# Three output stores placed behind two crossbar turns, and one tile turned one output piece sooner

## The chip, the core and the metric

The kernel runs on one core of a Trainium2 chip. The metric is the device time of one execution in microseconds; lower is better. Inside the core, TensorE (PE in the profile; its weight loads are listed as PEld), VectorE (DVE), ScalarE (ACT), GpSimd (POOL) and SyncE (SP) each run their own list of instructions in order and wait for each other through semaphores. Transfers are issued by SP and POOL and carried out by 16 DMA engines.

## The reference

Causal linear attention with a decay for each head, followed by a feed-forward layer with a snake activation:

```python
gamma = 1.0 - 2.0 ** (-5.0 - np.arange(H))                 # q, k, v: (4, 8, 768, 64)
for t in range(S):
    state = gamma[None, :, None, None] * state + np.einsum('bhd,bhe->bhde', k[:, :, t], v[:, :, t])
    y[:, :, t] = (1.0 / np.sqrt(D)) * np.einsum('bhd,bhde->bhe', q[:, :, t], state)
x = y.transpose(0, 2, 1, 3).reshape(B * S, H * D)          # 3072 x 512
h = x @ w_in                                               # 512 x 2048
s = np.sin(alpha * h)
out = (h + s * s / (alpha + 1e-09)) @ w_out                # 2048 x 512
```

## The kernel before

The 3072 tokens are cut into 24 tiles of 128 tokens. `P` (the list `order`) gives their order in time: P[0] to P[3] are the first tiles of the four batches, then come the other tiles of the batches. The tiles are grouped for the feed-forward layer: group 0 is P[0] to P[3], groups 1 to 8 have two tiles each (group 1 is P[4] and P[5], group 2 is P[6] and P[7], and so on), and the last group has four.

A tile passes these steps. Its q and k rows are loaded into `qkr` and v into `vr`, by transfers that POOL issues (`load_chunk`, profile lines L101 and L103). Then q and k are turned, so that the head dimension lies on the partitions; the result is the tile `qkT`. There are two ways to turn. For P[4] to P[7], `stage_T` does it on TensorE with 16 transposes (L281) and a copy of the result out of PSUM by ACT (L283) or DVE (L285). From P[8] on, `turn` does it through the crossbar of the DMA engines (`dma_start_transpose`, issued by SP, L290). After that `burst(old, new)` works on two neighbouring tiles at once on TensorE: for the tile `old` the products with the carried state (L365), the products with the scores (L438) and the sums for the state (L445); for the tile `new` its scores (L380), which read the `qkT` of `new`. The output of `burst` goes to `xT` by DVE (L487, "exit"), and the state goes to `s_f` and `s_q`.

The feed-forward layer of a group takes `xT` as input. `Slot` multiplies a column block of `w_in` with `xT` (L603), ACT takes the sine (L606) and the square (L611), and DVE adds the two parts into `gT` (L618). `ff_out` multiplies one of the 16 slices of `gT` with `w_out` for one tile (L628); one such matmul is called an output piece below. After the sixteenth piece `take` copies the tile's output from PSUM to a buffer `o_sb` (ACT L642 or DVE L640, five buffers) and issues its store on SP (L643).

The order on every engine is written out by hand (`tc.manual_schedule`). For group 0 and the passage to group 1 it is a long list of calls: the pieces of tiles P[2] and P[3] are laid one by one (`fill(n)` puts the next n of them) between the turns and bursts of P[4], P[5] and P[6]. The lines of this place:

```python
    run(fresh, "keep", "hand", "mask")
    fill(2)
    F((0, 1), (14,))
    F((0, 1), (15,))
    run(fresh, "exit")
    ...
    fill(1)
    stage_T(P[6], nc.scalar, "mm")
    fill(3)
    run(burst(P[5], P[6]), "exit", "keep", "hand", "mask")
    fill(4)
```

Group 1 then runs in `phase(1, ...)`, where `stage_T(P[7])` stands after the first slot, the crossbar turns of P[8], P[9] and P[10] after the second, third and sixth, and the bursts P[6]/P[7] and P[7]/P[8] in the third and sixth slot. The bursts P[8]/P[9] and P[9]/P[10] stand in `phase(2, ...)`.

On SP there is one list for stores and crossbar turns. The stores of the first three tiles of group 0 that are finished (P[2], P[0], P[1]) are issued as soon as `take` is called, ahead of the turns of P[8], P[9] and P[10].

Of the kernel before, what the change touches and what calls it, by code (L numbers as in the profile page):

```python
# [12 lines left out]
AFTER = mybir.DependencyInfo(mybir.DependencyClass.Sync, mybir.DependencyReason.DATA)  # L13


@with_exitstack
def kernel(
# [116 lines left out]
    def load_w_in(i, h=None):  # L134
        c = slice(i * fw, (i + 1) * fw) if h is None else slice(i * fw + h * fw // 2, i * fw + (h + 1) * fw // 2)
        nc.gpsimd.dma_start(out=w_in[:, :, c], in_=w_in_v[:, :, c])  # L136
# [28 lines left out]
    load_chunk(0, "v")  # L165
    load_chunk(order[1])
    load_chunk(order[2])
    for h in range(2):
        load_w_in(0, h)
    tok = consts.tile([128, NCH, 2], F32, name="tok")  # L170
    for b in range(2):
        nc.gpsimd.iota(tok[64 * b:64 * b + 64], pattern=[[C, NCH], [64, 2]], channel_multiplier=1, base=0,
                       allow_small_or_imprecise_dtypes=True)
    load_chunk(order[3], "qk")
    load_w_out(0, 0)
    load_chunk(order[3], "v")
    load_w_out(0, 1)
    for h in range(2):
        load_w_in(1, h)
    for h in range(2):  # L180
        load_w_out(1, h)
        load_w_in(2, h)


# [76 lines left out]
    def half_T(j, i, eng, bank=None):  # L261
# [7 lines left out]
        if eng is nc.scalar:  # L269
            nc.scalar.copy(o, pt)  # L270
        else:
            nc.vector.tensor_copy(o, pt)

    def stage_T(j, eng=None, tag="two"):
        pt = psum.tile([128, 2 * NP, 128], BF16, name="pt", tag=tag, bufs=4 if tag == "mm" else 1)
        st["qkT", j] = work.tile([128, 2 * NP, 128], BF16, name="qkT", tag="qkT", bufs=6)
# [5 lines left out]
        if eng is nc.scalar:  # L282
            nc.scalar.copy(st["qkT", j], pt)  # L283
        else:
            nc.vector.tensor_copy(st["qkT", j], pt)  # L285
# [7 lines left out]
    def stage_A(j, parts=1):  # L293
# [7 lines left out]
        aT = st["aT", j] = work.tile([128, 2, NP, 128], BF16, name="aT", tag="aT", bufs=3)  # L301
        if parts == 1:
            nc.vector.tensor_mul(aT.rearrange("p e n t -> p (e n) t"), pa.rearrange("p e n t -> p (e n) t"),  # L303
                                 dec.rearrange("p e n t -> p (e n) t"))
            return
        for h in range(2):
            c = slice(2 * h, 2 * h + 2)
# [22 lines left out]
    def stage_M(j, bank, parts=1):  # L330

        aT, vs = st["aT", j], raw["v", j]
        py = bank.rearrange("i (p t) -> i p t", p=NP)
        for h in range(parts):
            ps = range(NP * h // parts, NP * (h + 1) // parts)
            if h:
                py = psum.tile([128, NP, 128], F32, name="pyh", tag="mm", bufs=4)
            for p in ps:
                for e in range(2):
                    nc.tensor.matmul(py[half(e), p, :], vs[:, 2 * p + e, :], aT[:, e, p, :],  # L340
                                     start=(p == ps[0]), stop=True, skip_group_check=True)
            c = slice(ps[0], ps[-1] + 1)
            (nc.scalar.copy if parts == 1 else nc.vector.tensor_copy)(x_of(j)[:, c], py[:, c])


# [243 lines left out]
    class Slot:  # L589
# [19 lines left out]
        def sq(self, eng):  # L609
            if eng == "A":  # L610
                nc.scalar.activation(out=self.s, in_=self.s, func=ACTF.Square)  # L611
            else:
                nc.vector.tensor_mul(self.s, self.s, self.s)
# [11 lines left out]
    def ff_out(g, ts, f):  # L625
# [4 lines left out]
        if f == FF - 1 and (g, ts) not in ((0, 0), (0, 1)):  # L630
            take(g, ts)

    def take(g, ts):
# [5 lines left out]
        elif g > 0 or ts == 1:  # L639
            nc.vector.tensor_copy(o_sb, po[g, ts])  # L640
        else:
            nc.scalar.copy(o_sb, po[g, ts])  # L642
# [28 lines left out]
    def idle_work(n):  # L671
        for _ in range(n):
            nc.tensor.matmul(spare["ps"], warm[:, :128], warm, start=True, stop=True)  # L673
# [6 lines left out]
    idle_work(9)  # L680
    nc.vector.tensor_copy(raw["q", 0], near["q"])
    half_T(e0, 0, nc.vector)
    nc.scalar.copy(raw["k", 0], near["k"])
    idle_work(2)
    nc.vector.tensor_mul(dec.rearrange("p e n t -> p (e n) t"), dec.rearrange("p e n t -> p (e n) t"), mask_bc)
    half_T(e0, 1, nc.scalar)
    nc.scalar.activation(out=kg, in_=expo, func=ACTF.Exp, scale=-1.0)
    for c in range(1, NCH):
        nc.scalar.activation(out=step[:, c, :], in_=lgp, func=ACTF.Exp, scale=float(C * c))
    idle_work(2)  # L690
    stage_A(e0)
    half_T(e1, 0, nc.scalar)
    grow(0)
    idle_work(1)
    half_T(e1, 1, nc.vector)
    nc.tensor.transpose(pal, alpha_row, ident_f)
    stage_M(e0, front[:, 0])
    later_tables()
    nc.scalar.copy(alpha_sb, pal)
    grow(1)  # L700
    stage_A(e1)
    nc.scalar.activation(out=kgq, in_=expoq, func=ACTF.Exp, scale=-1.0)
    idle_work(1)
    half_T(e2, 0, nc.scalar)
    grow(2)
    idle_work(2)
    half_T(e2, 1, nc.vector)
    grow(3)
    stage_M(e1, front[:, 0])
    nc.scalar.activation(out=tiny, in_=warm[:, 0:1], func=ACTF.Sin)  # L710
    stage_A(e2, 2)
    idle_work(3)
    stage_M(e2, front[:, 0], 2)
    nc.vector.tensor_scalar_add(rec_alpha, pal, 1e-9)
    nc.vector.reciprocal(rec_alpha, rec_alpha)
    idle_work(2)
    scale_v(e0, nc.vector)
    for h in range(2):
        decay_table(2 * h + 1)
        decay_table(2 * h + 2)  # L720
        load_w_out(2, h)
        load_w_in(3, h)
    load_w_out(3, 0)
    load_chunk(order[4])
    load_chunk(order[5], "qk")
    load_w_out(3, 1)
    load_chunk(order[5], "v")
    decay_table(5)
    load_chunk(order[6])


    rest = [{}]

    def phase(g, outs, att, nf=1, on_vector=(), tags={}, early=()):
# [3 lines left out]
        for n in range(FF // nf):  # L738
# [13 lines left out]
            run(fresh, *(("keep", "hand", "exit") if g == 1 else ("mask", "keep0")))  # L752
            if fresh:
                rest[0] = fresh
            while done < min(no, no * (n + 1) * nf // (FF - 2 * (g == 1))):
# [7 lines left out]
            if g == 1:  # L763
                run(fresh, "mask")
# [11 lines left out]
    def F(ts, fs):  # L776
        for f in fs:
            for t in ts:
                ff_out(0, t, f)
        if FF - 1 in fs:  # L780
            for t in ts:
                take(0, t)

    def early(f, tag="mm"):
        return Slot(0, f, (0, n3), tag=tag)

    outs = out_pieces(0, (2, 3))[6:]

    def fill(n):
        for _ in range(n):  # L790
            outs.pop(0)()

    fourth = psum.tile([128, 2, 512], BF16, name="fourth", tag="two", padded_shape=[128, 2, 1024])
    a = early(0).sq("A")
    b = early(1).sq("A")
    half_T(e3, 0, nc.vector, fourth[:, 0])
    c = early(2).sq("A")
    a.add()
    half_T(e3, 1, nc.vector, fourth[:, 1])
    d = early(3).sq("A")  # L800
    b.add()
    stage_A(e3)
    both = psum.tile([128, 2, d_model], F32, name="po", tag="two")
    po[0, 0], po[0, 1] = both[:, 0], both[:, 1]
    F((0, 1, 2), (0, 1))
    c.add()
    stage_M(e3, psum.tile([128, 2, 512], F32, name="pye", tag="pa")[:, 0])
    copies = first_state(e0)
    d.add()
    copies()  # L810
    F((0, 1, 2), (2,))
    a = Slot(0, 0, (n3, n4), 4, "pa")
    F((0, 1, 2), (3,))
    a.sq("A").add()
    a = Slot(0, 4).sq("A")
    for f in range(5, FF):
        b = Slot(0, f, tag="pa" if f in (7, 10) else "mm")
        if f % 2 == 0 or f in (7, 11, 15):
            b.sq("A")
        if f % 2 == 0 and f - 1 not in (7, 11, 15):  # L820
            a.sq("D")
        a.add()
        a = b
        if f > 6:
            F((0, 1, 2) if f < 9 else (0, 1), (f - 3,))
        if f in (7, 9, 11):
            scale_v({7: e1, 9: e3, 11: e2}[f], nc.vector)
    scale_v(P[4], nc.gpsimd)
    stage_T(P[4], nc.vector, "pa")
    F((0, 1), (13,))  # L830
    fill(3)
    a.add()
    fill(1)
    m4 = scores(P[4])["mask"]
    stage_T(P[5], nc.scalar, "mm")
    m4()
    fill(6)
    scale_v(P[5], nc.vector)
    fresh = burst(P[4], P[5], apart=True)
    run(fresh, "keep", "hand", "mask")  # L840
    fill(2)
    F((0, 1), (14,))
    F((0, 1), (15,))
    run(fresh, "exit")


    load_chunk(P[7], "qk")
    load_chunk(P[8], "qk")
    scale_v(P[6], nc.gpsimd)
    load_chunk(P[7], "v")  # L850
    load_chunk(P[9], "qk")
# [103 lines left out]
```

## Time and profile before

| | |
|---|---|
| median of 3 runs | 208.54 us (208.07 to 210.15) |
| the profiled execution: time, and span from first to last instruction | 208.83 us, 206.8 us |
| TensorE busy | 200.2 us, 97% of the span |
| DVE, ACT, POOL busy | 153.0, 152.1, 124.1 us |
| granted TensorE clock | 1.00 |
| DMA moved | 24.79 MB, mean 120 GB/s |

The profile was taken in an execution of 208.83 us, 2.03 us more than its span of 206.8 us; this rest lies outside the first and last instruction. Busy time adds up what an engine spent in instructions. A matmul's row gives its start, and the start of the next row says how long TensorE stayed with it, because matmuls overlap: the durations of matmuls are longer than the distance between their starts. The chain that ended last tells which engine's work followed which up to the end.

### The profile page before, as it was taken

Reading aid. Unit: us, or ns where it says so; the run is one execution under the profiler, and the core shown is the slowest. Engines: PE = TensorE matmul, PEld = TensorE weight load, DVE = VectorE, ACT = ScalarE, POOL = GpSimd, SP = SyncE. Lnnn points to the kernel's source line nnn. Section 1 sums busy time; section 2 is a strip of 40 time slices with the busy share of each in tenths; the row PEclk is TensorE's granted clock in tenths of the full one; section 3 lists DMA queues with packets and bytes.
Section 4 is the critical chain, followed back from the end, with each engine's and each line's share of the span. In section 5 each row is a group of like instructions: output and inputs, shape, how many; then the busy total and the mean of one; then the engine's idle time right before and its main releaser. Section 6 shows DMA issues by size and latency. Waiting matters only on the chain.

```text
span 206.8 us, 5804 instructions
## 1 busy us (share of the span) xinstructions
PE 200.2 (97%) x2367; PEld 123.7 (60%) x2367; DVE 153.0 (74%) x323; ACT 152.1 (74%) x311; POOL 124.1 (60%) x172
## 2 busy tenths in 40 slices
PE   7699999999999999999999999999999999999994
PEld 2345544557766666766766676766766654444453
DVE  5688499767999988878879695975978975656220
ACT  7588888656997787787787778688686779999001
POOL 8998987999799996899486909990220000000000
PEclk9999999999999999999999999999999999999999
DMA  8999999999999999999995999992412101010212
GB/s 128 153 182 192 201 200 173 167 199 181 122 167 120 101 175 178 172 135 156 170 143 60 122 110 139 123 144 59 105 52 53 55 0 52 0 51 3 101 51 101
DMA packets 102906, 24.79 MB, mean 120 GB/s; under 512 B 93360, under 2 KB 99936, under 8 KB 102880
## 3 DMA queue, kind: packets, MB, share of 16 engines
q0 software_dynamic: 80080, 13.38, 89.8%
q1 hardware_dynamic: 22656, 10.99, 25.4%
q8 instruction: 18, 0.29, 0.6%
q10 hardware_dynamic: 144, 0.07, 0.1%
q14 instruction: 8, 0.07, 0.1%
HBM read 27.30 MB, written 6.29 MB: 162 GB/s over the span
## 4 chain that ended last, share of the span: by engine, by line
PE 88%; ACT 4%; DMA 3%; DVE 2%; issue 1%; SPq 0%
PE po L628 39%; PE ph L603 38%; DMA o_sb<-in_k_dram 3%; PE poh L653 2%; ACT s L606 2%; PE py L365 1%; ACT s L611 1%; PE pt L281 1%; PE py L429 1%; PE pa L380 1%; DVE gT L618 1%; DVE aT L308 1%; DVE aT L303 1%; PE pa L387 1%; PE pa L299 1%; PE py L438 1%
## 5 line engine op out<-in xcount | busy, mean ns | idle before, releaser
L618 DVE SCALAR_TENSOR_TENSOR gT<-s,rec_alpha,ph 128x256 bf16<-128x256 f32 (+3 forms) x164 | 79.8, 522 | 29.2 <-ACT s L611 28.8
L603 PE MATMUL ph<-xT,w_in 128*128 128x256 bf16 (+3 forms) x656 | 98.6, 291 | 0.3 <-DVE gT L618 0.3
L606 ACT ACTIVATE s<-ph,alpha_sb 128x256 f32<-128x256 f32 (+3 forms) x164 | 75.9, 505 | 26.4 <-PE ph L603 23.0
L628 PE MATMUL po<-w_out,gT 128*128 128x512 bf16 x368 | 95.2, 380 | 0.0
L603 PEld LDWEIGHTS <-w_in 128*128 128x128 bf16 x656 | 63.3, 98 | 33.3 <-issue 0.9
L611 ACT ACTIVATE s<-s 128x512 f32<-128x512 f32 (+1 forms) x94 | 58.8, 625 | 3.0
L628 PEld LDWEIGHTS <-gT 128*128 128x128 bf16 x368 | 34.2, 98 | 30.2 <-DVE gT L618 0.5
L125 POOL DMA_DIRECT2D qk_seq<-in_q_dram x32 | 21.6, 760 | 3.4 <-DMA v_seq<-in_v_dram 3.4
L125 POOL DMA_DIRECT2D qk_seq<-in_k_dram x32 | 21.3, 728 | 3.7 <-DMA qk_seq<-in_q_dram 3.5
L640 DVE COPY o_sb<-po 128x512 f32<-128x512 f32 x20 | 13.8, 688 | 9.4 <-PE po L628 9.0
L125 POOL DMA_DIRECT2D v_seq<-in_v_dram x24 | 16.9, 792 | 0.2
L163 POOL TENSOR_TENSOR v_seq<-v_seq,kgq 128x512 bf16<-128x512 bf16 x10 | 10.2, 1044 | 5.0 <-DMA v_seq<-in_v_dram 5.0
L103 POOL DMA_DIRECT2D vr<-in_v_dram x11 | 10.5, 951 | 0.8 <-DMA w_in<-in_moe_w_in_dram 0.6
L399 DVE TENSOR_TENSOR aTw<-pa,maskq 128x768 bf16<-128x768 f32 x10 | 9.5, 954 | 0.0
L487 DVE TENSOR_TENSOR xT<-py,qg 128x512 bf16<-128x512 f32 x13 | 8.9, 683 | 0.6 <-PE py L445 0.6
L657 ACT COPY o_sb<-poh 128x256 f32<-128x256 f32 (+1 forms) x2 | 0.6, 318 | 11.7 <-PE poh L653 11.7
L673 PE MATMUL spare<-warm 128*128 128x512 bf16 x22 | 8.0, 485 | 1.2 <-DVE warm L186 1.2
L513 POOL CAST s_q<-s_f 128x256 bf16<-128x256 f32 x1 | 0.4, 396 | 14.2 <-DVE s_f L507 14.2
L383 DVE TENSOR_TENSOR aT<-pa,mask 128x1024 bf16<-128x1024 f32 x7 | 8.5, 1219 | 0.4 <-PE pa L380 0.4
L513 ACT CAST s_q<-s_f 128x256 bf16<-128x256 f32 x12 | 4.7, 392 | 3.1 <-DVE s_f L507 2.6
L136 POOL DMA_DIRECT2D w_in<-in_moe_w_in_dram x8 | 6.3, 800 | 0.5 <-DMA w_out<-in_moe_w_out_dram 0.5
L103 POOL DMA_DIRECT2D qkr<-in_k_dram x7 | 6.3, 896 | 0.4 <-DMA w_in<-in_moe_w_in_dram 0.4
(123 smaller groups left out, 173.0 us busy)
## 6 DMA issues: line engine op xcount, KB each, us to landing
out_dram<-o_sb SPq DMA_DIRECT2D x23, 256.0 KB, 2.5
w_in<-in_moe_w_in_dram POOLq DMA_DIRECT2D x8, 256.0 KB, 7.9
w_out<-in_moe_w_out_dram POOLq DMA_DIRECT2D x8, 256.0 KB, 7.9
vr<-in_v_dram POOLq DMA_DIRECT2D x11, 128.0 KB, 5.6
v_seq<-in_v_dram POOLq DMA_DIRECT2D x16, 80.0 KB, 4.4
qkr<-in_q_dram POOLq DMA_DIRECT2D x7, 128.0 KB, 5.9
qkr<-in_k_dram POOLq DMA_DIRECT2D x7, 128.0 KB, 6.1
qk_seq<-in_q_dram POOLq DMA_DIRECT2D x16, 48.0 KB, 3.4
```

The source lines that it names most:

```text
L103: nc.gpsimd.dma_start(out=t, in_=chunk_of(src, j))
L125: nc.gpsimd.dma_start(out=o, in_=src[bt, head(b, m, e), now[0] * C:(now[-1] + 1) * C, :].rearrange("(f i) d -> i f d", i=64))
L163: eng.tensor_mul(t, t, by[:, j % NCH, :, None].to_broadcast([128, H, D]))
L383: return {"mask": lambda: nc.vector.tensor_mul(aT.rearrange("p e n t -> p (e n) t"), pa.rearrange("p e (n t) -> p (e n) t", n=NP), mask_bc)}
L399: return {"mask": lambda: nc.vector.tensor_mul(aT, pa[:, :, 0:384].rearrange("p e (m t) -> p e m t", m=2), maskq[:, None, None, :].to_broa ...
L487: nc.vector.tensor_mul(o, st["pyw", old][:, :, 0:256].rearrange("p b (m t) -> p b m t", m=2), by)
L603: nc.tensor.matmul(self.ph[:, m, :], w_in[:, i, f * 128:(f + 1) * 128], xT[g][:, i, self.lo:self.hi], start=(m == 0 and i == 0), stop=(i = ...
L606: nc.scalar.activation(out=self.s[:, m, :], in_=self.ph[:, m, :], func=ACTF.Sin, scale=alpha_sb[:, f:f + 1])
L611: nc.scalar.activation(out=self.s, in_=self.s, func=ACTF.Square)
L618: nc.vector.scalar_tensor_tensor(gT[self.g][:, f, self.lo:self.hi], self.s[:, m, :], rec_alpha[:, f:f + 1], self.ph[:, m, :], op0=ALU.mult ...
L628: nc.tensor.matmul(po[g, ts], gT[g][:, f, ts * C:(ts + 1) * C], w_out[:, f, :], start=(f == 0), stop=(f == FF - 1))
L640: nc.vector.tensor_copy(o_sb, po[g, ts])
```

## The change

Two things move. First, the list of calls for group 0, for the passage to group 1 and for group 1 itself is replaced by a table of words, `PLAN`, which `act` carries out one by one; nearly every word stands where its call stood. `stage_T`, `half_T`, `stage_A` and `stage_M` are split so that the PSUM copy is a word of its own, and `take` no longer issues the store when it is told which engine copies; the store is the word `G`. Second, two of the words stand elsewhere: the word that turns P[6] on TensorE (`T.6.mm`) stands ahead of the piece `F.3.2`, and the stores `G.2 G.0 G.1` stand behind the crossbar turns `X.8` and `X.9`.

```diff
+PLAN = """
...
+keep.4 hand.4 mask.4 F.3.0 F.3.1 F.01.14 F.01.15 O.0.A O.1.D exit.4 L.7.q L.7.k L.8.q L.8.k V.6.P L.7.v L.9.q
+L.9.k L.8.v V.7.P L.10.q L.10.k L.9.v V.8.P T.6.mm C.6.A F.3.2 F.3.3 F.3.4 F.3.5 U.5 exit.5 keep.5 hand.5 mask.5
+F.3.6 F.3.7 F.3.8 F.3.9 S.1:0.mm Q.1:0.A T.7.two C.7.D A.1:0 S.1:1.mm Q.1:1.A X.8 F.3.10 A.1:1 S.1:2.mm Q.1:2.A
+X.9 G.2 G.0 G.1 U.6 keep.6 hand.6 exit.6 F.3.11 A.1:2 mask.6 S.1:3.mm Q.1:3.A F.3.12 A.1:3 S.1:4.mm Q.1:4.A
+F.3.13 A.1:4 S.1:5.mm Q.1:5.A U.7 X.10 keep.7 hand.7 exit.7 F.3.14 A.1:5 mask.7 S.1:6.mm Q.1:6.A F.3.15 O.3.A
+G.3 A.1:6 S.1:7.mm Q.1:7.A A.1:7
+"""
...
-    def take(g, ts):
+    def take(g, ts, by=None):
...
+        if by is not None:
+            return o_sb
         nc.sync.dma_start(out=out_view[:, groups[g][ts], :], in_=o_sb)
...
+        elif op == "F":
+            for t in a[0]:
+                ff_out(0, int(t), int(a[1]))
+        elif op == "O":
+            aside["O" + a[0]] = take(0, int(a[0]), eng(a[1]))
+        elif op == "G":
+            nc.sync.dma_start(out=out_view[:, groups[0][int(a[0])], :], in_=aside.pop("O" + a[0]))
...
+        elif op == "T":
+            aside[a[0]] = stage_T(P[int(a[0])], a[1])
+        elif op == "C":
+            aside.pop(a[0])(eng(a[1]))
+        elif op == "X":
+            turn(P[int(a[0])])
...
-    fill(1)
-    stage_T(P[6], nc.scalar, "mm")
-    fill(3)
-    run(burst(P[5], P[6]), "exit", "keep", "hand", "mask")
-    fill(4)
```

The first place is on TensorE, at the turn of P[6]. `po_412` is the output of P[1], `po_747` (now `po_746`) that of P[3], `pt` the PSUM tile of the turn, and `py` the output of the burst P[5]/P[6]. Before, the turn's 16 pairs of weight load and transpose (one pair is shown) stand behind the third piece of P[3], and three more pieces of P[3] come between it and the burst:

```order
L628 MATMUL po_412<-w_out_70,gT_355 128x512
L628 LDWEIGHTS gT_355
L628 MATMUL po_747<-w_out_70,gT_355 128x512
L281 LDWEIGHTS qkr_349
L281 MATMUL pt_866<-ident_120,qkr_349 64x128
...
L365 LDWEIGHTS s_q0_170
L365 MATMUL py_888<-qkT_652,s_q0_170 64x128
```

With the change the turn follows the last piece of P[1] directly, and four pieces of P[3] come between it and the burst:

```order
L632 MATMUL po_412<-w_out_70,gT_355 128x512
L287 LDWEIGHTS qkr_350
L287 MATMUL pt_786<-ident_91,qkr_350 64x128
...
L632 MATMUL po_746<-w_out_70,gT_355 128x512
L369 LDWEIGHTS s_q0_141
L369 MATMUL py_809<-qkT_652,s_q0_141 64x128
```

One weight load and one matmul moved from ahead of the turn to behind it; nothing else on TensorE stands elsewhere.

The second place is SP's list. `qkr_765`, `qkr_773` and `qkr_781` are the loaded q and k of P[8], P[9] and P[10] (now `qkr_762`, `qkr_770` and `qkr_778`). Before, the three stores stand ahead of all turns:

```order
L151 DMA alpha_row_79<-in_moe_alpha_dram 16x128
L643 DMA out_0_dram<-o_sb_677 128x512
L643 DMA out_0_dram<-o_sb_754 128x512
L643 DMA out_0_dram<-o_sb_757 128x512
L290 DMA_TRANSPOSE qkT_1004<-qkr_765 128x8x128
L290 DMA_TRANSPOSE qkT_1022<-qkr_773 128x8x128
L290 DMA_TRANSPOSE qkT_1197<-qkr_781 128x8x128
L643 DMA out_0_dram<-o_sb_1220 128x512
```

With the change they stand between the second and the third turn:

```order
L173 DMA alpha_row_79<-in_moe_alpha_dram 16x128
L293 DMA_TRANSPOSE qkT_925<-qkr_762 128x8x128
L293 DMA_TRANSPOSE qkT_943<-qkr_770 128x8x128
L763 DMA out_0_dram<-o_sb_677 128x512
L763 DMA out_0_dram<-o_sb_753 128x512
L763 DMA out_0_dram<-o_sb_755 128x512
L293 DMA_TRANSPOSE qkT_1121<-qkr_778 128x8x128
L763 DMA out_0_dram<-o_sb_1144 128x512
```

Two turns moved past three stores. DVE, ACT and POOL carry out the same instructions in the same order as before.

More of the change, by code (lines that the diff above doesn't have):

```diff
@@ L163, in scale_v, with number_tokens @@
         eng.tensor_mul(t, t, by[:, j % NCH, :, None].to_broadcast([128, H, D]))
[L165 to L169, printed above, removed]
-    tok = consts.tile([128, NCH, 2], F32, name="tok")
[L171 to L182, printed above, removed]
+    tok = consts.tile([128, NCH, 2], F32, name="tok")
+    def number_tokens():
+        for b in range(2):
+            nc.gpsimd.iota(tok[64 * b:64 * b + 64], pattern=[[C, NCH], [64, 2]], channel_multiplier=1, base=0,
+                           allow_small_or_imprecise_dtypes=True)
     warm = consts.tile([128, 512], BF16, name="warm")
@@ L268, in half_T, with stage_T @@
         o = st["qkT", j][:, i * NP:(i + 1) * NP, :]
[L269 to L274, printed above, removed]
+        return lambda by: by.copy(o, pt) if by is nc.scalar else by.tensor_copy(o, pt)
+    def stage_T(j, tag):
         pt = psum.tile([128, 2 * NP, 128], BF16, name="pt", tag=tag, bufs=4 if tag == "mm" else 1)
-        st["qkT", j] = work.tile([128, 2 * NP, 128], BF16, name="qkT", tag="qkT", bufs=6)
+        qkT = st["qkT", j] = work.tile([128, 2 * NP, 128], BF16, name="qkT", tag="qkT", bufs=6)
         for i in range(2):
@@ L281, in stage_T @@
                     nc.tensor.transpose(pt[half(e), i * NP + p, :], raw["qk"[i], j][:, h, :], ident)
[L282 to L285, printed above, removed]
+        return lambda by: by.copy(qkT, pt) if by is nc.scalar else by.tensor_copy(qkT, pt)
     def turn(j):
@@ L300, in stage_A, with decayed @@
                                  start=(p == 0), stop=True, skip_group_check=True)
-        aT = st["aT", j] = work.tile([128, 2, NP, 128], BF16, name="aT", tag="aT", bufs=3)
-        if parts == 1:
+        return pa
+    def decayed(j, pa, c):
+        if ("aT", j) not in st:
+            st["aT", j] = work.tile([128, 2, NP, 128], BF16, name="aT", tag="aT", bufs=3)
+        aT = st["aT", j]
+        if c.stop - c.start == NP:
             nc.vector.tensor_mul(aT.rearrange("p e n t -> p (e n) t"), pa.rearrange("p e n t -> p (e n) t"),
                                  dec.rearrange("p e n t -> p (e n) t"))
-            return
-        for h in range(2):
-            c = slice(2 * h, 2 * h + 2)
+        else:
             nc.vector.tensor_mul(aT[:, :, c], pa[:, :, c], dec[:, :, c])
@@ L328, in x_of, with mixed @@
         return xT[g][:, :, i * C:(i + 1) * C]
-    def stage_M(j, bank, parts=1):
+    def mixed(j, part, bank=None):
         aT, vs = st["aT", j], raw["v", j]
+        if bank is None:
+            bank = front[:, 0] if part != "1" else psum.tile([128, 512], F32, name="pyh", tag="mm", bufs=4)
         py = bank.rearrange("i (p t) -> i p t", p=NP)
[L334 to L343, printed above, removed]
+        ps = {"-": range(NP), "0": range(2), "1": range(2, NP)}[part]
+        for p in ps:
+            for e in range(2):
+                nc.tensor.matmul(py[half(e), p, :], vs[:, 2 * p + e, :], aT[:, e, p, :],
+                                 start=(p == ps[0]), stop=True, skip_group_check=True)
+        c = slice(ps[0], ps[-1] + 1)
+        o = x_of(j)[:, c]
+        return lambda by: by.copy(o, py[:, c]) if by is nc.scalar else by.tensor_copy(o, py[:, c])
     tiles4 = [(b, e) for b in range(2) for e in range(2)]
@@ L629, in ff_out @@
                          start=(f == 0), stop=(f == FF - 1))
-        if f == FF - 1 and (g, ts) not in ((0, 0), (0, 1)):
+        if f == FF - 1 and g > 0:
             take(g, ts)
-    def take(g, ts):
+    def take(g, ts, by=None):
         o_sb = work.tile([128, d_model], F32, name="o_sb", tag="o_sb", bufs=5)
@@ L638, in take @@
             nc.scalar.copy(o_sb[:, h:], po[g, ts][:, h:])
-        elif g > 0 or ts == 1:
+        elif by is nc.scalar:
+            nc.scalar.copy(o_sb, po[g, ts])
+        else:
             nc.vector.tensor_copy(o_sb, po[g, ts])
-        else:
-            nc.scalar.copy(o_sb, po[g, ts])
+        if by is not None:
+            return o_sb
         nc.sync.dma_start(out=out_view[:, groups[g][ts], :], in_=o_sb)
@@ L669, with idle_work @@
     spare = {"ps": psum.tile([128, 512], F32, name="spare", tag="mm", bufs=4)}
-    def idle_work(n):
+    def idle_work(n, cols=512):
         for _ in range(n):
-            nc.tensor.matmul(spare["ps"], warm[:, :128], warm, start=True, stop=True)
+            nc.tensor.matmul(spare["ps"][:, :cols], warm[:, :128], warm[:, :cols], start=True, stop=True)
     def grow(p):
@@ L679 @@
     e0, e1, e2, e3 = order[:B]
[L680 to L729, printed above, removed]
     rest = [{}]
@@ L751, in phase @@
                 now.add()
-            run(fresh, *(("keep", "hand", "exit") if g == 1 else ("mask", "keep0")))
+            run(fresh, "mask", "keep0")
             if fresh:
                 rest[0] = fresh
-            while done < min(no, no * (n + 1) * nf // (FF - 2 * (g == 1))):
+            while done < min(no, no * (n + 1) * nf // FF):
                 outs[done]()
@@ L775 @@
     n3, n4 = 3 * C, 4 * C
[L776 to L794, printed above, removed]
@@ L812 @@
[L812 to L827, printed above, removed]
@@ L828 @@
-    scale_v(P[4], nc.gpsimd)
-    stage_T(P[4], nc.vector, "pa")
-    F((0, 1), (13,))
-    fill(3)
-    a.add()
-    fill(1)
[L834 to L850, printed above, removed]
@@ L857 @@
+    for word in PLAN.split():
+        act(word)
     load_seq(1, "q")
@@ L867 @@
         scale_v(j, nc.gpsimd)
-    fill(1)
-    stage_T(P[6], nc.scalar, "mm")
-    fill(3)
-    run(burst(P[5], P[6]), "exit", "keep", "hand", "mask")
-    fill(4)
-    where = {7: (1, 2), 8: (1, 5)}
+    where = {}
     for g in range(2, 6):
@@ L888, in B @@
         return lambda: burst(old, new, first, beside=beside, second=second)
-    at((1, 0), lambda: stage_T(P[7]))
-    for n in (8, 9):
-        at((1, n - 7), X(P[n]))
-    for n in range(7, 17):
+    for n in range(9, 17):
         new = P[n]
```

149 lines of the change are left out of this document (116 added, 33 removed).

## Prediction

> **What bounds the kernel now.** I read the page first: busy times, the slices, the chain that ended last. Then the waits of TensorE from 14 us on, to see how much of its time can be won at all.
>
> ```profile
> span 206.8 us, 5804 instructions
> PE 200.2 (97%) x2367; PEld 123.7 (60%) x2367; DVE 153.0 (74%) x323; ACT 152.1 (74%) x311; POOL 124.1 (60%) x172
> PE   7699999999999999999999999999999999999994
> PE 88%; ACT 4%; DMA 3%; DVE 2%; issue 1%; SPq 0%
> ```
>
> ```profile
> PE ph L603 <- DVE gT L618: 0.3, 1, 0.3
> PE pyh L340 <- DVE aT L308: 0.2, 1, 0.2
> ```
>
> TensorE sets the time: 97% of the span, 88% of the chain, and the only slices under nine tenths are the first two and the last. The second fence is all that the view of TensorE's waits has between 14 and 205 us: 0.5 us. Nothing that the change touches lies ahead of 43 us or behind the first store after the third turn, so a gain of over 1% (2.1 us) has no idle time from which it could come. A loss needs a new wait of TensorE.
>
> **The turn of P[6].** TensorE's rows around it, then two plain pieces and two plain bursts for comparison (start, duration):
>
> ```profile
> 44.19 0.64 PE L281 MATMUL pt<-ident,qkr 128*64 128x128 bf16 x16
> 44.76 0.82 PE L628 MATMUL po<-w_out,gT 128*128 128x512 bf16 x3
> 45.51 0.31 PE L365 MATMUL py<-qkT,s_q 64*64 64x128 bf16 x8
> ...
> 46.45 1.04 PE L628 MATMUL po<-w_out,gT 128*128 128x512 bf16 x4
> 47.39 1.03 PE L603 MATMUL ph<-xT,w_in 128*128 128x256 bf16 x8
> ...
> 50.99 0.31 PE L365 MATMUL py<-qkT,s_q 64*64 64x128 bf16 x8
> ...
> 51.85 0.39 PE L628 MATMUL po<-w_out,gT 128*128 128x512 bf16 x1
> 52.07 1.04 PE L603 MATMUL ph<-xT,w_in 128*128 128x256 bf16 x8
> ...
> 58.71 1.03 PE L603 MATMUL ph<-xT,w_in 128*128 128x256 bf16 x8 [0.28 <-DVE gT L618]
> ```
>
> A burst takes from its first L365 to the piece behind it. The burst P[6]/P[7] takes 51.85 - 50.99 = 0.86 us, the burst P[5]/P[6] takes 46.45 - 45.51 = 0.94 us with the same instructions. So 0.08 us are lost inside the second, too short to be listed as a wait. The weight loads and ACT's rows say where:
>
> ```profile
> 45.50 0.14 PEld L365 LDWEIGHTS <-s_q 64*64 64x64 bf16 x8 [0.42 <-issue]
> ...
> 45.93 0.26 PEld L380 LDWEIGHTS <-qkT 64*64 64x64 bf16 x16
> ...
> 50.99 0.15 PEld L365 LDWEIGHTS <-s_q 64*64 64x64 bf16 x8 [0.21 <-ACT s L606]
> ...
> 51.22 0.12 PEld L380 LDWEIGHTS <-qkT 64*64 64x64 bf16 x2
> ```
>
> ```profile
> 44.08 0.59 ACT L642 COPY o_sb<-po 128x512 f32<-128x512 f32 x1 [0.48 <-PE po L628]
> 44.86 1.01 ACT L283 COPY qkT<-pt 128x1024 bf16<-128x1024 bf16 x1 [0.20 <-PE pt L281]
> ```
>
> The scores' first weight load comes 0.23 us after the burst's start where it is free, 0.43 us after it here. ACT's copy of the turn ends at 44.86 + 1.01 = 45.87, and the load starts 0.06 us later. The scores wait for that copy.
>
> **What the move is worth.** One piece goes behind the turn; its price is one start to the next, 52.07 - 51.85 = 0.22 us. The turn is done 0.22 us sooner. ACT could follow by 0.19 us, because its copy of an output ends at 44.08 + 0.59 = 44.67 and the turn's copy started at 44.86. The copy then ends at 45.68, and with the same 0.06 us the load may start at 45.74; the free burst would want it at 45.50 + 0.23 = 45.73. So the stall goes but for 0.01 us: I take 0.08 us. Bounds: 0 if ACT gains nothing, 0.08 if the burst becomes a free one. A loss here is excluded by the order: the same pieces fill the same stretch, and the turn's data must be loaded 0.22 us earlier, while the stretch just ahead of it holds no wait of the weight loads for a transfer.
>
> Does the 0.08 us reach the end? The next visible wait is at 58.71 (0.28 us, for DVE's gT, behind ACT). ACT's chain to there starts with the first slot of group 1, whose matmuls at 47.39 come straight after the four pieces behind the burst. They and all behind them move along. Yes.
>
> **The stores and the turns of P[8] and P[9].** SP's rows, then three answers for one turn each (P[8], P[9], P[10]), then the weight loads that need them:
>
> ```profile
> 42.43 3.31 SPq L643 DMA_DIRECT2D out_dram<-o_sb  x3
> 47.48 11.69 SPq L290 DMA_TRANSPOSE qkT<-qkr  x3
> 59.62 0.43 SPq L643 DMA_DIRECT2D out_dram<-o_sb  x1
> ...
> 75.61 0.33 SPq L643 DMA_DIRECT2D out_dram<-o_sb  x1
> ```
>
> ```profile
> L290 SPq DMA_TRANSPOSE qkT<-qkr x1: 1327/1327/1327, 47.5 to 47.5; - x1
> DMA to landing us min/median/max: 7.6/7.6/7.6
> ...
> L290 SPq DMA_TRANSPOSE qkT<-qkr x1: 1232/1232/1232, 55.7 to 55.7; - x1
> DMA to landing us min/median/max: 4.2/4.2/4.2
> ...
> L290 SPq DMA_TRANSPOSE qkT<-qkr x1: 1792/1792/1792, 57.4 to 57.4; - x1
> DMA to landing us min/median/max: 4.8/4.8/4.8
> ```
>
> ```profile
> 55.45 0.12 PEld L380 LDWEIGHTS <-qkT 64*64 64x64 bf16 x2
> ...
> 61.82 0.12 PEld L380 LDWEIGHTS <-qkT 64*64 64x64 bf16 x2
> ...
> 69.73 0.12 PEld L380 LDWEIGHTS <-qkT 64*64 64x64 bf16 x2
> ```
>
> P[8] lands at 47.5 + 7.6 = 55.1 and is read at 55.45: 0.35 us to spare. P[9] lands at 59.9, read at 61.82: 1.9 us. P[10] lands at 62.2, read at 69.73: 7.5 us. TensorE waits for none of them, so landing sooner wins nothing; only lateness counts.
>
> The hardware queue q1 that carries stores and turns, in three stretches (44 to 49, 49.5 to 52, 52 to 55 us; packets, MB):
>
> ```profile
> q1 hardware_dynamic: 427, 0.78, 44.1%
> ...
> q1 hardware_dynamic: 1002, 0.26, 88.3%
> ...
> q1 hardware_dynamic: 54, 0.01, 3.3%
> ```
>
> The stores' 0.78 MB in large packets hold the queue to 49 us; the small packets of P[8]'s turn, issued at 47.48, come only then and are gone by 52. With the change no store is in front of it. Its issue waits for P[8]'s loads, which no longer share the engines with stores: 47.5 or sooner. Bounds for its landing: 55.1 as now, 47.5 + 3.1 = 50.6 with the shortest turn of the trace:
>
> ```profile
> DMA to landing us min/median/max: 3.1/5.6/8.7
> ```
>
> I take about 53; needed at 55.37. Cost 0. P[9]: issue at 55.7 or sooner, as its loads share with fewer stores; I take 59.9 or less; needed at 61.74. Cost 0. The stores: issued after P[9]'s turn, and P[10]'s turn behind them. They held the queue for 5 us (44 to 49), so P[10] lands by 62.2 + 5 = 67.2, needed at 69.65. Cost 0, with 2.4 us of cover left; each microsecond beyond it would be a microsecond of TensorE. SP's three store issues (3.31 us with their waits) stand before that turn only. No engine waits for these stores until a buffer comes round: there are five, two used by the first inputs, so it is the third output after them that needs the first of their buffers. Its store is the one at 75.61, some 10 us after these stores are likely to land.
>
> The Trainium skill, page "DMA: Bandwidth & Descriptors", section "Queues, rings and completion order", has two rules here. One says that each DMA engine takes the descriptors of a ring in order, and SP has one row of rings; the three stretches agree. The other says that a completion is a strongly ordered write that waits for all earlier writes of its engine, of other queues too; the trace fits it, since P[8]'s packets were gone by 52 and it landed at 55.1. That rule speaks against the change: a turn can be held up by loads however its own queue is ordered.
>
> **Sum.** 208.83 - 0.08 + 0 = 208.75 us for an execution like the profiled one. That one lies 0.29 us above the median of 208.54; against the median it is 208.46. I give 208.5.
>
> **Rivals.** (1) The turn is sooner and the stall stays: ACT takes up the copy no earlier, because the output copy in front of it ends only at 44.67 and its hand-over costs what is won. For it: the 0.01 us left in my sum. Against it: the 0.20 us for which ACT sat idle. Time 208.83, by the median 208.5.
>
> (2) More is won than the stall: with P[8]'s and P[9]'s data early, POOL's waits go (the row below, in 43 to 60 us), transfers run ahead, and the 0.28 us at 58.71 go as well. Against: that wait is ACT's and DVE's, which read no transfer there. Time 208.83 - 0.08 - 0.28 = 208.47, by the median 208.2.
>
> ```profile
> POOL vr L163 <- DMA vr<-in_v_dram: 1.8, 2, 1.3
> ```
>
> (3) Slower: P[9]'s turn lands late. The place is the weight load at 61.74; it decides from a landing 6.0 us after an issue at 55.7. P[8]'s turn shows the mechanism: packets gone by 52, landing 3.1 us later while loads went on. With this tail on P[9], 59.9 + 3.1 = 63.0, that is 1.3 us late: 208.75 + 1.3 = 210.0. With the longest turn (8.7), 64.4, 2.7 late: 211.4. Against it: P[9] landed in 4.2 us, and now too has no store in front of it; the stores come behind. By the strongly ordered rule named above the time would be this rival's, not another.
>
> **How the numbers follow.** The forecast gets 0.58, rival 1 0.14, rival 2 0.08, rival 3 0.20, because the spare time of 1.9 us is less than the turns' spread of 3.1 to 8.7. About 1% is what a measurement of this kernel can tell from no change: the three runs shown spread by 2.08 us. Half of rival 3 (0.10) lies above 1%, and the spread of the runs can put 0.04 above and 0.03 below the bound whatever the cause. So faster 0.03, within 1% 0.83, slower 0.14. The range starts 0.4 us under the lowest run (208.07), rival 2's gain, at 207.7, and ends at 210.1, which takes in the highest run shown less 0.08 and the lesser half of rival 3.
>
> **What would show it.** Right: in the profile after, the burst P[5]/P[6] takes 0.86 us instead of 0.94; ACT's copy of the turn starts straight after its output copy; the turn of P[8] is issued by 47.5 and lands before 55; the stores are issued after the turn of P[9]; TensorE's wait at about 58.6 remains. Wrong: a wait of the weight loads L380 for a transfer at about 61.7 or 69.6 (rival 3, or the third turn behind the stores), a burst of 0.94 us (rival 1), or no wait at 58.6 (rival 2). A difference that appears far from 43 to 70 us would mean that I have overlooked something.

## The result: slower by 0.4%, and the loss lies where nothing was moved

| | before | after |
|---|---|---|
| median of 22 runs each | 208.44 us (208.07 to 210.15) | 209.72 us (208.37 to 214.73) |
| ratio after to before, 95% interval | | 1.0038 (1.0020 to 1.0056) |
| profiled execution, span | 208.83 us, 206.8 us | 212.62 us, 210.5 us |

The change is slower, by 0.8 us according to the ratio, and it scatters more: 10 of its 22 executions took over 210 us, against one of 22 before. The ratio leaves out the four executions of the change that took over 211.5 us, the profiled one among them; so its trace is read for where the time can go, not for how much is lost on average.

The page after, lines that answer to those of before:

```profile
span 210.5 us, 5806 instructions
PE 200.4 (95%) x2367; PEld 123.7 (59%) x2367; DVE 153.2 (73%) x323; ACT 152.1 (72%) x311; POOL 124.1 (59%) x172
PE   7799999999999979999995999999999999999994
PE 45%; POOL 26%; DMA 25%; issue 2%; DVE 0%; POOLq 0%
```

TensorE is busy for the same 200 us. Two slices have fallen, the one that ends at 79 us to seven tenths and the one from 110 to 116 us to five. The chain that ended last was 88% TensorE; now half of it is POOL and DMA. TensorE's waits from 14 to 205 us have two new rows (total, times, longest, in us):

```profile
PE pa L417 <- POOL v_seq L185: 2.2, 1, 2.2
PE pa L391 <- DMA qkT<-qk_seq: 1.4, 1, 1.4
```

They lie at 79 and 112 us, both outside the turns that the prediction priced.

**The turn of P[6].** TensorE, its weight loads, then ACT in the trace after:

```profile
43.90 0.64 PE L287 MATMUL pt<-ident,qkr 128*64 128x128 bf16 x16
44.47 1.04 PE L632 MATMUL po<-w_out,gT 128*128 128x512 bf16 x4
45.43 0.31 PE L369 MATMUL py<-qkT,s_q 64*64 64x128 bf16 x8
...
46.29 1.04 PE L632 MATMUL po<-w_out,gT 128*128 128x512 bf16 x4
```

```profile
45.67 0.12 PEld L384 LDWEIGHTS <-qkT 64*64 64x64 bf16 x2
```

```profile
44.00 0.59 ACT L644 COPY o_sb<-po 128x512 f32<-128x512 f32 x1 [0.48 <-PE po L632]
44.58 1.01 ACT L288 COPY qkT<-pt 128x1024 bf16<-128x1024 bf16 x1
```

ACT's copy of the turn follows its output copy at once and ends at 45.59. The burst takes 46.29 - 45.43 = 0.86 us, as the free one did, and its scores start 0.24 us after it. Everything up to 77 us runs 0.16 us ahead of before (the wait for gT stands at 58.55 instead of 58.71).

**SP's list** after:

```profile
48.01 8.28 SPq L293 DMA_TRANSPOSE qkT<-qkr  x2
56.35 3.30 SPq L763 DMA_DIRECT2D out_dram<-o_sb  x3
59.88 1.44 SPq L293 DMA_TRANSPOSE qkT<-qkr  x1
61.41 0.55 SPq L763 DMA_DIRECT2D out_dram<-o_sb  x1
```

The three stores start 14 us later than before, at 56.35 instead of 42.43. P[10]'s turn stands behind them and lands 8.7 us after its issue, at 68.6, still before its use at 69.56.

**POOL's loads** of the first sequence tiles (eight for q, eight for k, 48 KB each) come next. POOL's rows before, then after, and the landing of the eight q loads in each:

```profile
57.15 5.33 POOL L125 DMA_DIRECT2D qk_seq<-in_q_dram  x8
62.38 5.36 POOL L125 DMA_DIRECT2D qk_seq<-in_k_dram  x8
67.55 1.08 POOL L103 DMA_DIRECT2D vr<-in_v_dram  x1
...
DMA to landing us min/median/max: 3.2/4.0/4.3
```

```profile
56.74 5.39 POOL L146 DMA_DIRECT2D qk_seq<-in_q_dram  x8
62.75 1.97 POOL L146 DMA_DIRECT2D qk_seq<-in_k_dram  x3 [0.61 <-DMA qk_seq<-in_q_dram]
65.23 0.66 POOL L146 DMA_DIRECT2D qk_seq<-in_k_dram  x1 [0.52 <-DMA qk_seq<-in_q_dram]
...
69.73 1.31 POOL L146 DMA_DIRECT2D qk_seq<-in_k_dram  x2 [1.95 <-DMA qk_seq<-in_q_dram]
71.02 0.92 POOL L124 DMA_DIRECT2D vr<-in_v_dram  x1
...
DMA to landing us min/median/max: 5.0/6.3/8.8
```

The k loads go to other buffers than the q loads, yet they wait for them: the trace gives the sixteen loads eight semaphores in turn, and a load that finds its semaphore in use waits for it. The chain that ended last, from 56 to 113 us (start, us, what), shows the pattern:

```profile
56.79 3.90 POOL qk_seq L146 x6
60.68 8.76 DMA qk_seq<-in_q_dram
69.44 0.28 issue
69.73 1.31 POOL qk_seq L146 x2
...
77.79 7.62 DMA qk_seq<-in_q_dram
...
85.70 6.75 DMA qk_seq<-in_k_dram
...
95.54 6.22 DMA v_seq<-in_v_dram
...
102.05 7.54 DMA qk_seq<-in_q_dram
...
111.72 1.08 POOL v_seq L185
112.84 0.32 PE pa L417 x16
```

The q load issued at 60.68 is the seventh; its landing at 69.44 releases the seventh k load at 69.73. A load waits for the landing of the load eight places ahead of it. With the stores' 0.78 MB on the way, the q loads land in 5.0 to 8.8 us instead of 3.2 to 4.3; from about 5 us on the list stalls, because POOL comes to the ninth load 5.2 us after the first (57.15 to 62.38 before). The last k load is issued at 70.38 instead of 66.91. These 3.5 us are not made up: from 57 to 112.8 us the chain runs through POOL and landings alone.

Two consumers on TensorE see it. The turn of P[11] needs these sequence tiles: it was issued at 69.96, is now issued at 73.11 and lands 6.0 us later, at 79.1. Its first reader in the burst P[10]/P[11], before, then the burst after:

```profile
77.66 0.23 PE L387 MATMUL pa<-qkT 64*64 64x128 bf16 x2
```

```profile
77.23 0.31 PE L369 MATMUL py<-qkT,s_q 64*64 64x128 bf16 x8
...
79.13 0.25 PE L391 MATMUL pa<-qkT 64*64 64x128 bf16 x4 [1.42 <-DMA qkT<-qk_seq]
...
79.60 0.60 PE L632 MATMUL po<-w_out,gT 128*128 128x512 bf16 x2
```

The other is POOL's own scaling of P[14]'s v, which stands behind the loads in POOL's list. POOL's scaling and TensorE's sums that read it, before and then after:

```profile
107.63 4.05 POOL L163 TENSOR_TENSOR v_seq<-v_seq,kgq 128x512 bf16<-128x512 bf16 x4
...
109.09 0.30 PE L413 MATMUL pa<-v_seq,qk_seq 64*64 64x64 bf16 x16
```

```profile
111.70 4.08 POOL L185 TENSOR_TENSOR v_seq<-v_seq,kgq 128x512 bf16<-128x512 bf16 x4
...
112.84 0.32 PE L417 MATMUL pa<-v_seq,qk_seq 64*64 64x64 bf16 x16 [2.24 <-POOL v_seq L185]
```

Before, the first of the four scalings ended at 107.63 + 4.05 / 4 = 108.64 and was read at 109.09: 0.45 us to spare. It is 4.1 us later now. The two waits, 1.42 + 2.24 = 3.66 us, are nearly all of the 3.7 us between the spans.

### The profile page after: what moved, and what is told of

Its sections match the earlier page's. It is cut to its first block, busy times and chain, and to the rows that moved or that the text cites. A ratio compares the mean times of both kernels' runs of the same rounds, so it can differ in the third digit from the quotient of the medians.

```text
span 210.5 us, 5806 instructions
## 1 busy us (share of the span) xinstructions
PE 200.4 (95%) x2367; PEld 123.7 (59%) x2367; DVE 153.2 (73%) x323; ACT 152.1 (72%) x311; POOL 124.1 (59%) x172
## 4 chain that ended last, share of the span: by engine, by line
PE 45%; POOL 26%; DMA 25%; issue 2%; DVE 0%; POOLq 0%
PE po L632 21%; PE ph L607 19%; DMA qk_seq<-in_q_dram 11%; DMA w_out<-in_moe_w_out_dram 5%; POOL qkr L124 4%; POOL v_seq L146 4%; POOL qk_seq L146 4%; DMA qk_seq<-in_k_dram 3%; POOL vr L124 3%; DMA v_seq<-in_v_dram 3%; POOL w_in L158 3%; DMA vr<-in_v_dram 3%; POOL qkr L122 3%; POOL w_out L162 2%; POOL qg L249 2%; PE poh L659 2%
## 5 line engine op out<-in xcount | busy, mean ns | idle before, releaser
L124 POOL DMA_DIRECT2D qkr<-in_q_dram x7 | 6.4, 920 | 1.4 <-DMA w_out<-in_moe_w_out_dram 1.2
```

The source lines that it names most:

```text
L124: nc.gpsimd.dma_start(out=t, in_=chunk_of(src, j))
```

## The experiments

The theory, called S below: the stores' data, moved among the sequence tiles' loads, put POOL's list back, and P[11]'s turn and P[14]'s v come late. Rivals: the sooner turn of P[6] hurts (T); P[10]'s turn behind the stores is the cause (H); any store moved costs the same (H2). Most edits are words of `PLAN`; they are shown against the change, as pieces of its lines (`...` marks what is left out). Runs of one group were compared with the kernel before on the same chip; its medians there were 208.87, 208.62 and 208.47 us. Each kernel ran 12 times, those of 4 and the repeat of the change 6 times.

**1. The piece alone: the stores go back to their places.**

```diff
-... F.2.12 F.2.13 F.2.14 F.2.15 O.2.A V.5.D U.4
+... F.2.12 F.2.13 F.2.14 F.2.15 O.2.A G.2 V.5.D U.4
-... F.01.14 F.01.15 O.0.A O.1.D exit.4 ...
+... F.01.14 F.01.15 O.0.A G.0 O.1.D G.1 exit.4 ...
-X.9 G.2 G.0 G.1 U.6 ...
+X.9 U.6 ...
```

> The turn of P[6] one piece sooner, the three stores back ahead of the crossbar turns. Theory S (the moved stores share the DMA engines with the loads of the sequence tiles from 57 us on, POOL's list of loads falls about 3 us behind, and TensorE then waits for the crossbar data of P[11] and for the scaled v of P[14]): nothing of that here, so 0.1 us faster than before, about 208.3, ratio 0.998 to 1.000, no wait near 79 and 112 us, POOL's load of the second half of the q and k of batch 1 ends at about 67 us as before. Rival T (the sooner turn is what hurts): slower than before like the change, ratio about 1.004, both waits there.

Measured: 208.63 us, ratio 0.998 (0.9947 to 1.0012). The profiled execution took 208.18 us (span 206.1); no wait at 79 or 112 us, last k load issued at 66.97. T falls: the sooner turn costs nothing that the interval could show. Whether it wins its 0.1 us, the interval cannot say.

**2. The stores alone: the piece goes back.**

```diff
-... V.8.P T.6.mm C.6.A F.3.2 F.3.3 ...
+... V.8.P F.3.2 T.6.mm C.6.A F.3.3 ...
```

> The three stores behind the turns of P[8] and P[9], the turn of P[6] where it was before. Theory S: as slow as the change or 0.1 us slower, ratio 1.003 to 1.008, with waits of 1 to 3 us near 79 or 112 us in many executions. Rival T: as fast as before, ratio 0.999 to 1.001.

Measured: 210.29 us, ratio 1.0057 (1.0019 to 1.0094). TensorE's waits behind 50 us:

```profile
PE pa L391 <- DMA qkT<-qk_seq: 1.7, 1, 1.7
PE pa L417 <- POOL v_seq L185: 0.8, 1, 0.8
```

The same two rows as in the change, without the piece. The stores are the cause.

This execution (212.65 us, span 210.6) shows a further loss. The granted clock of TensorE was 0.50 from 79.5 to 82.5 us, right behind the wait for P[11]'s turn; the row of the clock in 40 slices has it in the slice from 79 us:

```profile
PEclk9999999999999996999999999999999999999999
```

The two waits are 2.5 of the 3.8 us between this span and that of before; 3 us at half the clock are worth 1.5 us by estimate, about the rest. The waits in the two traces of the change, 1.42 and 2.24, 1.74 and 0.7 us, had no such drop behind them; what decides it stays open.

**3. No stores, run twice.** The change with the three stores left out: the output tiles of P[0], P[1] and P[2] are never written.

```diff
-X.9 G.2 G.0 G.1 U.6 ...
+X.9 U.6 ...
```

> The change without its three stores: the outputs of P[0], P[1] and P[2] are never written, everything else is as in the change, so the third crossbar turn follows the second directly. Theory S: no data of stores among the loads, so POOL's loads of batch 1 end by 67 us, no wait at 79 and 112 us, about 208.2, ratio 0.997 to 1.000, with less spread than before. Rival N (the executions of the change were late for a reason other than the stores, such as an early load that lands 1 us late): the waits stay in some executions, ratio above 1.002.

Measured: 209.12 us, ratio 1.0019 (0.9990 to 1.0048). The trace has no wait at 79 or 112 us and the last k load at 67.05, but the time decides nothing: the profiled execution, 209.95 us, lost 1.49 us at 19.5 us waiting for `w_out`, ahead of all that differs. So it ran again:

> The change with the three stores of P[2], P[0] and P[1] left out (these three output tiles are never written), a second time: the first gave 1.0019 with an interval from 0.999 to 1.0048, which decides nothing, though its trace had no wait at 79 or 112 us. Theory S: 0.995 to 1.000, the last k load of batch 1 by 67.2 us, no wait at 79 or 112 us. If something else in the change costs the time (the piece, the table of words): 1.003 or more again, as the change itself.

Measured: 208.74 us, ratio 1.0006 (0.9980 to 1.0031); last k load at 66.50, no wait at 79 or 112 us. The ratio lies just over what S expected, with 1.000 well inside the interval, and the rival's 1.003 at its edge. In both traces the waits are gone with the data.

**4. The stores later still,** behind P[10]'s turn, which gets its old place.

```diff
-X.9 G.2 G.0 G.1 U.6 ...
+X.9 U.6 ...
-... U.7 X.10 keep.7 ...
+... U.7 X.10 G.2 G.0 G.1 keep.7 ...
```

> The three stores behind the third crossbar turn too (that of P[10]). Theory S with the amount of data as the cause: the same 0.78 MB run among the loads a little later, so about as slow as the change, ratio 1.002 to 1.008. Rival H (what hurts is that the turn of P[10] stands behind the three stores on SP's queue and moves its data late): the turn of P[10] lands by about 63 us as before, the loads are not late, ratio about 1.000.

Measured: 211.78 us, ratio 1.0125 (1.0066 to 1.0184), the worst of all and above what S expected, from six executions that spread from 208.83 to 212.37 us. The turn of P[10] lands at 62.68 as before, so H falls. The only trace is of the shortest execution. In it the sixteen loads are hardly late (last k load at 66.47); POOL waits 1.7 us for a landing just behind them, and TensorE 0.4 us for P[14]'s v. Where the longer ones lose their 3 us, no trace shows.

**5. One store moved,** P[1]'s; P[2]'s and P[0]'s at their old places.

```diff
-X.9 G.2 G.0 G.1 U.6 ...
+X.9 G.1 U.6 ...
```

> The change with only one of the three stores (that of P[1]) behind the turns of P[8] and P[9]; those of P[2] and P[0] stand ahead of them as before. Theory S (amount of data among the loads): a third of the data is moved, POOL's last load of q and k of batch 1 is about 1 us late instead of 3 to 3.5, which the cover of P[11]'s turn (3 us) hides and that of P[14]'s scaled v (0.5 us) does not, so between e1_piece_only and the change: 208.6 to 209.2, ratio 0.999 to 1.004. Rival H2 (any store between the second and third turn costs the same): as slow as the change.

Measured: 208.76 us, ratio 1.0003 (0.9982 to 1.0024). H2 falls. The last k load, at 67.13, is 0.2 us later than before and not the 1 us that S expected; there is no wait for P[14]'s v.

**6. Two stores moved,** P[0]'s and P[1]'s; P[2]'s at its old place.

```diff
-X.9 G.2 G.0 G.1 U.6 ...
+X.9 G.0 G.1 U.6 ...
```

> The change with P[2]'s store back at its old place; only the stores of P[0] and P[1] (0.52 MB) stand behind P[9]'s turn. With one store moved the last k load of batch 1 was issued at 67.1 us and the ratio was 1.0003; with three it is issued after 69 us and the ratio is 1.004 to 1.009. Theory S (dose): two thirds of the data, last k load at 68 to 69.5 us, ratio 1.001 to 1.005, the wait at 79 us under 1 us. A rival (a threshold: POOL's list absorbs any two stores, and only the third fills it up): ratio as with one, 0.998 to 1.002, last k load by 67.5 us.

Measured: 209.45 us, ratio 1.0031 (1.0003 to 1.0060). POOL's rows:

```profile
55.40 5.33 POOL L146 DMA_DIRECT2D qk_seq<-in_q_dram  x8
61.88 0.66 POOL L146 DMA_DIRECT2D qk_seq<-in_k_dram  x1 [1.15 <-DMA qk_seq<-in_q_dram]
```

The ratio lies between those of one store and of three, as a dose would have it, but the intervals overlap, and this one does not exclude the threshold rival (1.002 at most). The last k load, at 67.06, is what that rival said, not S: the list took 11.66 us, 1.9 longer than before, but started 1.75 us sooner in this execution. So dose or threshold stays open. There is no wait at 79 us and one of 0.7 us for P[14]'s v.

**7. The stores between the turns of P[8] and P[9].**

```diff
-... A.1:0 S.1:1.mm Q.1:1.A X.8 F.3.10 ...
+... A.1:0 S.1:1.mm Q.1:1.A X.8 G.2 G.0 G.1 F.3.10 ...
-X.9 G.2 G.0 G.1 U.6 ...
+X.9 U.6 ...
```

> The change with the three stores issued between the turns of P[8] and P[9], that is some 6 us sooner than in the change and some 5 us later than before (at about 48 to 51 us). Theory S (the stores' 0.78 MB among the sequence tiles' loads put POOL's loads back by 3 us): the lateness is in between, because the data are through by about 56 us, when the first load of batch 1's sequence tiles is only being issued; the last k load of batch 1 is issued by 68 us, no wait of TensorE at 79 or 112 us, ratio 0.997 to 1.002. What can go wrong instead is P[9]'s turn, which now has the stores in front of it: it lands later than 60 us and is needed at 61.7. Theory O (what matters is only whether a store stands ahead of a turn or behind it, not where its data run): here the stores stand behind P[8]'s turn as in the change, so it should cost as the change does, ratio 1.004 to 1.009, with the last k load after 69 us.

Measured: 208.49 us, ratio 1.0003 (0.9984 to 1.0022). The stores go at 50.2 to 52.1 and land by 57.9; the q loads start at 58.82 and land in 3.5 to 5.1 us; the list takes 9.92 us without a stall:

```profile
58.82 5.33 POOL L146 DMA_DIRECT2D qk_seq<-in_q_dram  x8
64.06 5.37 POOL L146 DMA_DIRECT2D qk_seq<-in_k_dram  x8
```

The stores stand behind a turn, as in the change, and cost nothing, so O falls: what counts is what their data meet. The last k load (68.74) and a wait of 1.2 us for P[14]'s v miss the expectation: in this execution all loads were late from 16 us on, where TensorE already waited 0.8 us for P[3]'s rows, and the scaling started at 109.84.

**8. The change with P[14]'s v scaled earlier,** between the q and the k loads of the last batch instead of behind both (its `scale_v` is taken out of the loop at the end of POOL's list and put ahead of the k loads).

> The change, with POOL's scaling of v of P[14] placed between its loads of q and k of batch 3, some 7 us sooner. Theory S: the loads stay late, the wait near 112 us for POOL's scaled v (2.4 us in the change's profile) goes, the wait near 79 us for P[11]'s turn stays; faster than the change by 0.5 to 2 us in the median, 208.6 to 209.5. Rival N (noise of single executions, no chain through POOL): no difference from the change.

Measured: 209.41 us, ratio 1.0030 (1.0004 to 1.0057). Its profiled execution, 210.58 us, lost 1.26 us at 19.7 us waiting for `w_out`, ahead of all that differs.

**The change once more,** in the same group:

> The change once more beside the others, for the median on this chip and another profile. Theory S: ratio 1.002 to 1.008; a profile with waits of TensorE near 79 or 112 us whenever POOL's last load of q and k of batch 1 is issued later than 69 us, and without them when it is issued by 68 us. Rival N: waits and the issue time do not go together.

Measured: 210.89 us, ratio 1.0091 (1.0058 to 1.0124), above the 1.008 that S allowed. Its profiled execution took 211.38 us, with the last k load at 70.90, 1.74 us of wait ending at 79.4 and 0.7 ending at 111.6; its eight q loads:

```profile
DMA to landing us min/median/max: 7.3/8.1/10.1
```

With the early scaling the wait for P[14]'s v is gone, the last k load is still late (69.72), and TensorE, some 1 us later in this execution than in that of before, waits 0.3 us at 79 us for P[11]'s turn. The median is 1.5 us under that of the change in the same group, and the two intervals just fail to meet. But the change itself gave 1.0038 in the first measurement, which the early scaling does not beat. So that wait is likely a part of the loss; how large a part, these runs do not show.

**9. The piece alone with the early scaling.**

> The turn of P[6] one piece sooner, stores in their old place, and v of P[14] scaled by POOL between the loads of q and k of batch 3. Theory S: the same fast executions as e1_piece_only (about 208.2 to 208.4) and fewer late ones, median 208.3 to 208.5, ratio 0.996 to 0.999. Rival N: no difference from e1_piece_only.

Measured: 209.05 us, ratio 1.0011 (0.9990 to 1.0033): no better than the piece alone, as rival N had it; S missed. Its profiled execution waits 1.1 us at 56.8 for P[8]'s turn. No version beat the kernel before beyond its interval.

Side by side, from the profiled execution of each (first q load to last k load, both at issue):

| kernel | list of 16 loads, us | that execution, us | ratio of the kernel |
|---|---|---|---|
| before | 9.75 | 208.83 | 1 |
| stores between P[8] and P[9] | 9.92 | 210.76 | 1.0003 |
| piece alone with early scaling | 10.11 | 209.83 | 1.0011 |
| one store moved | 10.12 | 208.91 | 1.0003 |
| no stores | 10.66, 10.51 | 209.95, 208.96 | 1.0019, 1.0006 |
| piece alone | 10.82 | 208.18 | 0.998 |
| stores behind P[10]'s turn | 11.00 | 208.83 | 1.0125 |
| two stores moved | 11.66 | 208.91 | 1.0031 |
| change with early scaling | 12.84 | 210.58 | 1.0030 |
| change | 13.63, 14.97 | 212.62, 211.38 | 1.0038, 1.0091 |
| stores alone | 13.94 | 212.65 | 1.0057 |

All with a list under 11 us are within their interval of no change; all above it are slower. The stores behind P[10]'s turn do not fit, with 11.00 us and the highest ratio; their one trace is of their shortest execution. The list does not give the time of a single execution: the one of 210.76 us had a list of 9.92 us, with all loads late from 16 us on, and the one of 208.91 us had 11.66 us. So the table agrees with the account above, but does not measure the loss.

## Why the prediction was wrong

**The turn of P[6]: right.** The burst fell from 0.94 to 0.86 us by the way described. Of the 0.16 us by which TensorE is ahead behind it, the other half was there before the burst began (45.43 instead of 45.51). Rivals 1 and 2 did not come: the stall went, and the 0.28 us at 58.55 stayed.

**The turns of P[8] and P[9]: right in the answer, not in the sizes.** P[8] was issued at 48.0 and landed at 54.65, not at 53. P[9] landed at 61.55 and is read at 61.65: the 1.9 us of cover had shrunk to 0.1. That it was still in time was luck. The turn took 6.5 us instead of 4.2; in the piece alone, with the stores ahead of the turns as before, it took 6.6 us, so the stores behind it are not needed to explain that. Rival 3 was a near miss in place, and is not where the time went. Its tail of 3.1 us was too long by up to 1 us: 54 of P[8]'s packets came after 52 us, all but two of them before 53.

**P[10]: right.** It landed at 68.6, not 67.2, with 1 us left.

**The stores, "Cost 0": this step failed.** It is the term of the sum that was off, and it was put at nothing because its list of consumers was too short. It listed as consumers of the moved transfers the three turns behind them and the five output buffers, and left out POOL's loads, which share the DMA engines with the stores. Before, the stores met the loads of single tiles at 42 to 49 us, and TensorE waited for none of these; with the change they met the list that feeds P[11]'s turn (3.0 us of cover: landing at 74.6, read at 77.66) and P[14]'s v (0.45 us). The term was 0. It measured 3.66 us of waits in the profiled execution, and 0.8 us for the whole change by the ratio. The rows that would have told it stood in the trace of before: q loads that land in up to 4.3 us while POOL comes to the ninth after 5.2 us, and the 0.45 us ahead of the sums at 109.09. Rival 2 named POOL's waits, but only those for `vr`, and as a possible gain.

The prediction used the strongly ordered completion from the Trainium skill ("DMA: Bandwidth & Descriptors", section "Queues, rings and completion order") for a turn held up by loads. Here it fits the other way round: loads held up by stores, 3.2 to 4.3 us becoming 5.0 to 8.8. Whether the ordered write or the sharing of the engines does it, no run here tells apart. The Trainium skill, on the same page, section "Anatomy of one DMA — SWDGE (gpsimd) path", gives 2.0 us plus the bytes at 436 GB/s for such a load, 2.1 us for 48 KB by estimate; no load of these eight was that quick, in either trace, so a plan made with it would have seen no danger.

"A difference that appears far from 43 to 70 us would mean that I have overlooked something" held: the waits stand at 79 and 112 us.

The median of 209.72 us lies inside the stated range, and the change within the 1% that got 0.83. That is luck: the range reached up to 210.1 us for the spread of the runs and for rival 3, and neither is what came. The direction was wrong: 0.08 us less was forecast. With 22 executions of each kernel the measurement could also tell apart much less than the 1% that the prediction took as its limit.

## What to carry to other kernels

A transfer that is moved has a cost where it arrives, on all the lists that share the DMA engines there, not only on its own queue: find the consumers of every load that is in flight in the new place, and their cover, down to the end of that list. A list of loads whose issue waits for earlier landings turns a longer landing into a delay that stays, as long as the list has no idle time; and an engine's own work queued behind its loads is one of the consumers. Where a store has to move, put it where its data are through before such a list begins (50 to 58 us here), not merely behind the next turn.

## What the runs showed that was not expected

- POOL had eight loads in flight at most in this stretch: one that had to wait was issued 0.28 us after the landing of the one eight ahead (69.44 to 69.73).
- A delay of 3.5 us at 70 us was still 4.1 us at 112 us, since in that trace the chain that ended last ran through POOL's list all the way.
- The executions differ early on: 1.49 and 1.26 us lost at 19.5 us for `w_out` in two runs, 0.8 us at 16.5 us for P[3]'s rows in another, with the same instructions up to there. So the margins read from one trace (0.45 us for P[14]'s v, 0.35 us for P[8]'s turn) are not there in every execution; P[8]'s turn was late in two of the profiled runs (one store moved 0.4 us, piece with early scaling 1.1 us), in both with stores still ahead of it.
- The mean granted clock was 0.991 or 0.992 in 10 of the 70 executions of the kernels with two or three stores moved behind P[9]'s turn, in one of the 72 of the other versions, and in none of the 87 of the kernel before that were timed beside them. The one of these with a trace, in experiment 2, shows half the clock right behind a wait. That the waits bring it about is likely, not shown.
